# Row-block projection of the first K, the first Q in score banks, and P*V moved to the next score visit, in a fused attention and gated-MLP kernel

## The chip, the cores and the metric

One NeuronCore of one Trainium2 chip. The metric is the device time of one execution in microseconds (us), the median over runs. A profile covers one execution, and its span (first to last instruction) is about 1.8 us shorter than that run's device time.

Engines: PE is TensorE (matmuls), PEld its weight loads, ACT ScalarE, DVE VectorE, POOL GpSimd, SP the engine that issues most DMA. L449 in a line of the profile is line 449 of that kernel's source.

## The reference, cut to what matters

```python
def reference(A_x, A_wq, A_wk, A_wv, A_wo, A_beta, B_x, B_w_gate, B_w_up, B_w_down, gate_w):
    # x: 2048 x 512; 32 heads of 16; four segments of 512 tokens
    q, k, v = x @ wq, x @ wk, x @ wv
    for s in range(4):
        a_dot = softmax(qs @ ks.T * scale + mask) @ vs     # causal, inside a segment
        a_mem = phi(qs) @ M / (phi(qs) @ z + 1e-6)         # memory of earlier segments
        o = g * a_mem + (1 - g) * a_dot
        M, z = M + phi(ks).T @ vs, z + phi(ks).sum()
    a = concat(o) @ wo
    b = (gelu(x @ w_gate) * (x @ w_up)) @ w_down           # 512 -> 1792 -> 512
    gate = sigmoid((x * gate_w).sum(-1))
    return gate * a + (1 - gate) * b
```

## The kernel before

The program is recorded as tasks, and a list scheduler written in the kernel's own Python gives each engine its order when the program is built. It keeps a simulated clock per engine, fed with hand-written estimates and one bias per task name. On the chip there is only the finished order; semaphores enforce its dependencies. So an edit of an estimate or a bias can reorder the whole kernel.

PE does two kinds of work: plain matmuls on the whole array, and *tiled* ones, which split it into four row or column groups (32\*128, and 128\*17 or 128\*32, in the timelines). Scores (`qk`) and P*V (`pv`) are tiled, and so is the memory update (`mz`). A *visit* is a run of tiled matmuls between two plain ones; a *hole* is a stretch in which PE stands still.

```python
PATIENCE = 3.0                      # how long a P*V waits for a score visit to join
# ... loads of the head
for c0, c1 in ((0, 128), (128, 512)):
    for key, w, src in (("wk", wk, A_wk), ("wq", wq, A_wq)):
        wdma((key, c0 > 0), SP, w[:, :, c0:c1], r4(src)[:, :, c0:c1], ...)
wdma("wv", SP, wv[:], r4(A_wv), 524288)
wdma("gwb", SP, gwb[:], gate_w.partition_broadcast(P), 131072)
wdma("beta", SP, betab[:], A_beta.partition_broadcast(P), 65536)
wdma(("wg", 0), SP, wg[:, :, 0:half], ...)      # first half of the columns of w_gate
wdma(("wg", 1), SP, wg[:, :, half:DF], ...)     # second half
xdma(1)                             # x of segment 1, transposed by DMA, four pieces
for i in range(7):                  # matmuls on a constant, while x is on its way
    gw = Grp(banks)
    n = 512 if i < 6 else 384
    task(f"warm{i}", PE, [Instr(lambda e, gw=gw, n=n: e.matmul(
        gw.f32()[:, 0:n], ones[:, 0:128], ones[:, 0:n], start=True, stop=True),
        [], [gw.key], 0.107 * n / 128)], grp=gw, bias=5000.0 - i)
# ... memory(s): 64 small matmuls, the task mz{s}
m = task(f"mz{s}", PE, [Instr(... e.matmul(..., tile_position=(0, 32 * c))) 
                        for t in range(4) for kt in range(4) for c in range(4)], grp=gm)
m.tiled = "pv"
m.patience = PATIENCE
# ... attention(s): 32 small matmuls per P*V, two per tile t
p = task(f"pv{s}_{t}_{j}", PE, instrs, grp=gp, after=joint)
p.tiled = "pv"
p.patience = 0.0 if t == 3 else PATIENCE        # the last of a segment does not wait
# ... the program
xdma(2, after=pk0); wdma(("wu", 0), ...); wdma(("wu", 1), ...); wdma("wd", ...); wdma("wo", ...)
# ... the end
for t in S.schedule():
    for ins in t.alts[t.eng]:
        em.plan(t.eng, ins)
```

(Cuts are marked with "...".)

The softmax here doesn't subtract the row's maximum and nothing guards it: scores larger than these inputs give would overflow.

Of the kernel before, what the change touches and what calls it, by code (L numbers as in the profile page):

```python
# [32 lines left out]
PV_JOIN = 0.11  # L33
# [3 lines left out]
    "D0": -705, "D1": -805, "D2": -380, "D3": -442, "G0": -222, "G1": -900, "G2": -744, "G3": -86, "GdT0": 97,  # L37
    "GdT1": 844, "GdT2": -1, "GdT3": 895, "Gev0": 862, "Gev1": -349, "K0": 777, "K1": -529, "K2": 250,
    "K3": 307, "Q0": 715, "Q1": -519, "Q2": 584, "Q3": -641, "U0": -844, "U1": -888, "U2": -53, "U3": -206,
    "Um0": 900, "Um1": 148, "Um2": 49, "Um3": -86, "V0": 318, "V1": -357, "V3": 539, "Vev0": 540, "Vev1": 758,  # L40
    "Vev2": 262, "Vev3": -72, "Vlo0": -900, "Vlo1": 900, "Vlo2": -70, "Vlo3": 237, "consts": 21, "exp0": -666,
    "exp1": 177, "exp2": -517, "exp3": -395, "exsT0": 77, "exsT1": -899, "exsT2": -94, "exsT3": 695, "fin0": 37,
    "fin1": -471, "fin2": 741, "fin3": -517, "gbd": -146, "gelu0": -795, "gelu1": 416, "gelu2": 1, "gelu3": 126,
    "gexp": 402, "gexs0": -594, "gexs1": -701, "gexs3": 76, "gmat": -900, "gmul1": 900, "gmul2": -10,
    "gmul3": 319, "gsum0": -318, "gsum1": -86, "gsum2": -613, "gsum3": -900, "gts0": 73, "gts1": -850,
    "gts2": -487, "gts3": 848, "ident": 503, "kl0": -826, "kl1": -900, "kl2": -661, "kl3": 900, "kp0": 509,
    "kp1": 3, "kp2": -900, "kp3": -405, "masks": 769, "msk0": -290, "msk1": 789, "msk2": 116, "msk3": -63,
    "mz0": -162, "mz1": 638, "mz2": -319, "mzacc0": -423, "mzacc1": 170, "mzacc2": 439, "mzbd0": -25,
    "mzbd1": -178, "mzbd2": 70, "norm0": 704, "norm1": -880, "norm2": -46, "norm3": 166, "num2": -887,
    "num3": -200, "nump1": -900, "nump2": -220, "nump3": -164, "oTd1": 896, "oTd2": 268, "oTd3": 899,  # L50
    "omg": 528, "out0": 408, "out1": -644, "out10": 2, "out11": 869, "out12": 745, "out13": 461, "out14": -25,
    "out15": -280, "out2": 230, "out3": -27, "out4": 313, "out5": -134, "out6": 284, "out7": -18, "out8": 682,
    "out9": -139, "pkT0": 5, "pkT1": 569, "pkT2": 281, "pkc0": 489, "pkc1": -900, "pkc2": -14, "pke0": 310,
    "pke1": 399, "pke2": -73, "pqc1": 496, "pqc2": 14, "pqc3": -117, "pqe1": -17, "pqe2": 649, "pqe3": 63,
    "pv0": -95, "pv1": -551, "pv2": -900, "pv3": 30, "pvt0": -169, "pvt1": 86, "pvt2": -513, "pvt3": -26,
    "qk0": 417, "qk1": 185, "qk2": 503, "qk3": 669, "tload": 355, "vones": -877, "w": -765, "warm0": 21,
    "warm1": 747, "warm2": -324, "warm3": 371, "warm4": 223, "warm5": -120, "warm6": -334, "x0": -96,
    "x0ev0": 93, "x0ev1": 23, "x0t0": 596, "x0t1": 606, "x1": 367, "x2": -181, "x3": -900, "xt1": 533,
    "xt2": -189, "xt3": 11
# [42 lines left out]
class Task:  # L102


    def __init__(self, name, alts, grp=None, after=(), bias=0.0, nbytes=0):
        self.name = name
        self.alts = alts
        self.grp = grp
        self.after = tuple(after)
        self.bias = bias + BIAS.get(name[:re.search(r"[_.]|$", name).start()], 0.0)  # L110
        self.nbytes = nbytes
        self.tiled = None
        self.patience = 0.0
        self.ahead = False
        self.est = {e: sum(i.est for i in l) for e, l in alts.items()}
        rs, ws = set(), set()
        for l in alts.values():
            for i in l:
                rs.update(i.reads)
                ws.update(i.writes)  # L120
        self.reads, self.writes = rs, ws
        self.preds, self.succs = set(), set()
        self.prio = 0.0
        self.eng = None
        self.start = self.finish = None
        self.id = None


class Sched:
# [32 lines left out]
    def schedule(self):  # L162
# [34 lines left out]
        last_pe = None  # L197
        while len(order) < n:
# [34 lines left out]
            if e == PE:  # L233
                if t.tiled == "pv" and last_pe == "pv":
                    t.finish -= PV_JOIN
                last_pe = t.tiled
# [137 lines left out]
def _build(es, nc, A_x, A_wq, A_wk, A_wv, A_wo, A_beta, B_w_gate, B_w_up, B_w_down, gate_w, out):  # L374
# [108 lines left out]
    rank = [9000.0]  # L483
# [5 lines left out]
    def wdma(key, eng, dst, src, nbytes, nonc=False, after=()):  # L489
        rank[0] -= 20.0  # L490
        dma("w_" + str(key), eng, lambda: dst, lambda: src, [], [("w", key)], nbytes, bias=rank[0], nonc=nonc,
            after=after)

    def xdma(s, after=()):
        for kb in range(4):
            rank[0] -= 20.0
            dma(f"x{s}_{kb}", SP, lambda kb=kb: xT[s % NX][:, kb, :],
                lambda kb=kb: A_x[0, s * 512:(s + 1) * 512, kb * 128:(kb + 1) * 128],
                [], xk(s, kb), 262144, issue=1.25, transpose=True, bias=rank[0] if s < 2 else 0.0,
                after=after)  # L500
# [10 lines left out]
              [("c", "ident")], [("c", "ident")], 0.3)], bias=9990.0)  # L511
    task("tload", ACT, [Instr(lambda e: e.activation(stmp[:, 0:1], ones[:, 0:1], ACTF.Exp), writes=[("stmp",)],
                              est=1.5)], bias=8000.0)
    xin = hT[1][:, 0:4, :]
    for a in range(4):
        rank[0] -= 20.0
        dma(f"x0_{a}", (SP, ACT)[a % 2], lambda a=a: xin[:, a, :], lambda a=a: A_x[0, a * 128:(a + 1) * 128, :], [],
            [("hT", 1, a)], 131072, bias=rank[0], issue=0.45)
    for c0, c1 in ((0, 128), (128, 512)):
        for key, w, src in (("wk", wk, A_wk), ("wq", wq, A_wq)):  # L520
            wdma((key, c0 > 0), SP, w[:, :, c0:c1], r4(src)[:, :, c0:c1], 1024 * (c1 - c0) * (2 if c0 == 0 else 1))
    wdma("wv", SP, wv[:], r4(A_wv), 524288)
    wdma("gwb", SP, gwb[:], gate_w.partition_broadcast(P), 131072)
    wdma("beta", SP, betab[:], A_beta.partition_broadcast(P), 65536)
    wdma(("wg", 0), SP, wg[:, :, 0:half], wgr[:, :, 0:half], 917504)
    wdma(("wg", 1), SP, wg[:, :, half:DF], wgr[:, :, half:DF], 917504)
    xdma(1)
# [23 lines left out]
    for g in range(4):  # L551
# [6 lines left out]
                               writes=[("Vaug", i, kt) for kt in range(4)], est=2.3) for i in range(2)]  # L558
         + [Instr(lambda e, j=j: e.memset(Vlow[j][:], 0.0), writes=[("Vlow", j)], est=2.3) for j in range(2)],
# [47 lines left out]
    def proj_T(name, s, t, w, wkey, dst, wkeys, even=None):  # L607

        g = Grp(banks)
        xs = xT[s % NX]  # L610
        nu = 2 if even is not None else 1
        cols = [slice(512 // nu * u, 512 // nu * (u + 1)) for u in range(nu)]
        pieces(name, g, [mm(g, lambda c=c: g.f32()[:, c], w[:, kb, t * 128:(t + 1) * 128], xs[:, kb, c],
                            [*(xk(s, kb)[u:u + 1] if nu > 1 else xk(s, kb)), ("w", (wkey, t > 0))],
                            kb == 0, kb == 3, 512 // nu)
                         for u, c in enumerate(cols) for kb in range(4)], 2 * nu)
        if even is not None:
            task(name + "even", ACT, [Instr(lambda e: e.activation(even[0], g.f32()[:, :], ACTF.Copy,
                                                                   scale=maskc[0][:, 0:1]),
                                            [g.key, ("c", "mask", 0)], [even[1]], act_t(512, ap=True))], grp=g)  # L620
        copy_out(name + "ev", g, lambda: dst[:, t, :], lambda: g.f32()[:, :], [g.key], wkeys, 512)

    def phi_task(nm, s, phase, src, skey, dst, dkey, i):
# [13 lines left out]
                  dk + [("pex",)], dk, 0.95)])  # L637

    def klow_tasks(s, tiles):
# [3 lines left out]
        for j in range(2):  # L643
# [6 lines left out]
                            rd, wr, act_t(n, False, ap=True))],  # L650
                DVE: [Instr(lambda e, dst=dst, src=src, j=j: e.tensor_scalar(dst, src, maskc[j][:, 0:1], None, ALU.mult),
                            rd, wr, dve_t(n, 1, ap=True))]}))

    def prep(s):
# [21 lines left out]
        for tile in range(4):  # L676
            g = Grp(banks)
            pieces(f"V{s}_{tile}", g, [mm(g, lambda g=g: g.f32()[:, :], xT[x3][:, kb, tile * 128:(tile + 1) * 128],
                                          wv[:, kb, :], [*xk(s, kb), ("w", "wv")], kb == 0, kb == 3, 512)
# [4 lines left out]
        for j in range(2):  # L684
            dma(f"Vlo{s}_{j}", SP, lambda j=j: Vlow[j][j:P:2], lambda j=j: Vaug[sl][0:64, :, j],
                [("Vaug", sl, tile) for tile in range(4)], [("Vlow", j)], 139264)
# [8 lines left out]
        for a in range(4):  # L695
# [3 lines left out]
                            [("gprod", s)] + xkeys, [("glog", s, a), ("gjunk", s, a)], act_t(512, False) + 0.1)],  # L699
# [13 lines left out]
            exsT[sl][32 * g:32 * g + 32, c:16:4], exs[32 * c:32 * c + 32, s4]), [("exs", s), ek], [ek], 0.22)  # L713
# [81 lines left out]
    def attention(s):  # L795
        sl = s % 2
        for t in range(4):
            def fill(name, steps, dst, key, masks):

                instrs = []  # L800
                for (lhs, rhs, c0, ncol, rd) in steps:
                    for g in range(4):
# [3 lines left out]
                            (0.2 / len(steps) + ncol / 2370.0 + (0.01 if ncol < 128 else 0.0)) / 4))  # L806
# [27 lines left out]
            def lows(t=t):  # L834
# [8 lines left out]
                masks = [(PTl[:].rearrange("p g (b c) -> p (g b) c", c=64), [[0, 32], [2, 64]], 1, 2048)]  # L843
                fill("L", steps, PTl, ("PTl",), masks)

            def pv(j, where, joint):
                gp = Grp(banks)
                instrs = []
                for kb in range(4):
                    slot, c0 = where[kb]  # L850
                    for q in range(4):
# [4 lines left out]
                            [("PT", slot), ("Vaug", sl, kb)], [gp.key], 0.0342))  # L856
# [9 lines left out]
                p.patience = 0.0 if t == 3 else PATIENCE  # L866
# [3 lines left out]
            def norm():  # L870
# [11 lines left out]
                          [("recip", i2), ("GdT", sl)], [("sc1", i2)], 0.34),  # L882
# [3 lines left out]
                if s > 0:  # L886
                    ins.append(Instr(lambda e, t=t: e.tensor_tensor(oT[sl][:, t, :], oT[sl][:, t, :], ott[:],
                                                                    ALU.add), ok + dk, ok, 0.7))
# [240 lines left out]
```

## Time and profile before

| | before |
|---|---|
| device time, first 3 runs | 268.4, 269.25, 270.0 us |
| span of the profile | 267.5 us |
| plain 512-column matmuls, start to start | 0.216 us |
| first score visit starts | 16.84 us |
| last matmul ends | 264.87 us |

The waits of PE in the kernel before: who waited, for what, us in total, times, longest.

```profile
PE psW L449 <- issue: 3.8, 24, 0.2
...
PE psW L449 <- ACT qT L463: 0.4, 1, 0.4
PE psW L449 <- ACT hT L937: 0.4, 1, 0.4
...
PE psW L449 <- DMA wk<-in_A_wk_dram: 0.3, 1, 0.3
```

No wait of weight. The 24 of 0.2 us are gaps where a matmul was not recorded (2965 recorded, 3005 built).

The timeline of PE before, around two later points of interest: start, duration, line, operation, output and inputs, count, and in brackets the idle time ahead with its cause.

```profile
18.48 1.03 PE L449 MATMUL psW<-xT,wg 128*128 128x512 bf16 x4
19.43 0.40 PE L803 MATMUL psXALL<-qT,kpad 32*128 32x320 bf16 x8
19.99 2.11 PE L449 MATMUL psW<-xT,wg 128*128 128x512 bf16 x9 [0.16 <-issue]
...
27.23 0.40 PE L803 MATMUL psXALL<-qT,kpad 32*128 32x320 bf16 x8
27.56 0.71 PE L769 MATMUL psW<-vaug,phkt 128*32 128x34 bf16 x64
28.43 1.67 PE L449 MATMUL psW<-xT,wq 128*128 128x512 bf16 x7 [0.16 <-DVE phq L632]
...
33.06 0.40 PE L803 MATMUL psXALL<-qT,kpad 32*128 32x320 bf16 x8
33.39 0.61 PE L852 MATMUL psW<-pt,vaug 128*17 128x448 bf16 x16
...
34.83 1.24 PE L449 MATMUL psW<-xT,wg 128*128 128x512 bf16 x5 [0.16 <-issue]
```

Every visit closes within 0.2 us. The 64 memory matmuls (L769) come at 27.56, in another visit than the first P*V (L852 and L860) at 33.39.

### The profile page before, as it was taken

Reading aid. Unit: us, or ns where it says so; the run is one execution under the profiler, and the core shown is the slowest. Engines: PE = TensorE matmul, PEld = TensorE weight load, DVE = VectorE, ACT = ScalarE, POOL = GpSimd, SP = SyncE. Lnnn points to the kernel's source line nnn. Section 1 sums busy time; section 2 is a strip of 40 time slices with the busy share of each in tenths; the row PEclk is TensorE's granted clock in tenths of the full one; section 3 lists DMA queues with packets and bytes.
Section 4 is the critical chain, followed back from the end, with each engine's and each line's share of the span. In section 5 each row is a group of like instructions: output and inputs, shape, how many; then the busy total and the mean of one; then the engine's idle time right before and its main releaser. Section 6 shows DMA issues by size and latency. Waiting matters only on the chain.

```text
span 267.5 us, 7093 instructions
## 1 busy us (share of the span) xinstructions
PE 257.9 (96%) x2965; PEld 118.4 (44%) x3005; DVE 199.9 (75%) x385; ACT 212.1 (79%) x188; POOL 102.3 (38%) x232
## 2 busy tenths in 40 slices
PE   8999999999999999999999999999999999999996
PEld 5444444344443443434354444444344444444354
DVE  1769799898989898889756877987952688753451
ACT  4889988899998997998858998887767767777602
POOL 8364553873002433485201433486300252352300
PEclk9999999999999999999999999999999999999999
DMA  6998992000203443000021224010020025001002
GB/s 192 228 328 184 390 241 42 1 2 0 44 0 79 81 101 102 22 20 2 0 44 39 42 59 124 21 44 2 0 44 0 2 59 42 0 22 36 8 0 78
DMA packets 33775, 18.22 MB, mean 68 GB/s; under 512 B 21456, under 2 KB 33744, under 8 KB 33744
## 3 DMA queue, kind: packets, MB, share of 16 engines
q1 hardware_dynamic: 33456, 17.51, 27.0%
q8 instruction: 23, 0.38, 0.6%
q10 hardware_dynamic: 288, 0.26, 0.3%
q14 instruction: 8, 0.07, 0.1%
HBM read 9.84 MB, written 2.10 MB: 45 GB/s over the span
## 4 chain that ended last, share of the span: by engine, by line
PE 84%; ACT 5%; DVE 3%; issue 3%; DMA 2%; POOL 1%; SPq 0%; ACTq 0%; DVEq 0%
PE psW L449 68%; PE psXALL L803 8%; PE psW L852 5%; ACT pt L810 3%; DMA wk<-in_A_wk_dram 2%; PE psXALL L449 1%; PE psW L860 1%; POOL exsT L712 1%; DVE tb L867 0%; PE psW L769 0%; ACT L937 0%; ACT L926 0%; SPq L480 0%; DVE mzbd L784 0%; DVE phkt L692 0%
## 5 line engine op out<-in xcount | busy, mean ns | idle before, releaser
L810 ACT ACTIVATE pt<-psXALL 128x2048 bf16<-128x2048 f32 x64 | 120.1, 1876 | 26.0 <-PE psXALL L803 23.9
L814 POOL TENSOR_SCALAR_AFFINE_SELECT pt<-pt 128x256 bf16<-128x256 bf16 x128 | 59.2, 464 | 131.6 <-ACT pt L810 126.6
L449 PE MATMUL psW<-xT,wu 128*128 128x512 bf16 x216 | 51.9, 380 | 0.8 <-issue 0.6
L449 PE MATMUL psW<-xT,wg 128*128 128x512 bf16 x214 | 50.2, 380 | 1.7 <-issue 1.3
L449 PE MATMUL psW<-wd,hT 128*128 128x512 bf16 x203 | 50.3, 380 | 0.9 <-issue 0.8
L958 DVE TENSOR_TENSOR hT<-psW,hT 128x512 bf16<-128x512 f32 x56 | 37.5, 684 | 11.4 <-PE psW L449 10.9
L449 PEld LDWEIGHTS psW<-xT,wg 128*128 128x128 bf16 x224 | 20.4, 98 | 25.7 <-issue 2.5
L449 PEld LDWEIGHTS psW<-xT,wu 128*128 128x128 bf16 x224 | 20.4, 98 | 24.5 <-issue 2.3
L867 DVE STREAM_TRANSPOSE tb<-psW 128x512 f32<-128x512 f32 x32 | 21.3, 697 | 12.6 <-PE psW L860 12.2
L449 PEld LDWEIGHTS psW<-wd,hT 128*128 128x128 bf16 x210 | 18.8, 98 | 22.5 <-issue 2.5
L803 PE MATMUL psXALL<-qT,kpad 32*128 32x320 bf16 (+3 forms) x512 | 25.8, 273 | 0.3 <-ACT pt L810 0.3
L937 ACT ACTIVATE hT<-psW 128x512 bf16<-128x512 f32 x28 | 15.9, 601 | 7.0 <-PE psW L449 6.9
L814 POOL TENSOR_SCALAR_AFFINE_SELECT ptl<-ptl 128x2048 bf16<-128x2048 bf16 x8 | 16.9, 2117 | 9.4 <-ACT ptl L810 9.0
L803 PEld LDWEIGHTS psXALL<-qT,kpad 32*128 32x128 bf16 x512 | 7.7, 92 | 27.6 <-ACT pt L810 19.6
L852 PE MATMUL psW<-pt,vaug 128*17 128x192 bf16 (+3 forms) x512 | 18.7, 273 | 0.0
L810 ACT ACTIVATE ptl<-psXALL 128x2048 bf16<-128x2048 f32 x8 | 15.0, 1876 | 3.6 <-PE psXALL L803 3.6
L449 PE MATMUL psW<-xT,wk 128*128 128x512 bf16 (+1 forms) x64 | 16.1, 376 | 0.8 <-issue 0.5
L712 POOL COPY exsT<-exs 32x4 f32<-32x4 f32 x64 | 15.4, 241 | 3.7
L466 DVE CAST hT<-psW 128x512 bf16<-128x512 f32 x21 | 14.1, 683 | 2.8 <-PE psW L449 2.5
L449 PE MATMUL psW<-wo,oT 128*128 128x512 bf16 x55 | 15.2, 380 | 0.5 <-issue 0.3
L449 PE MATMUL psW<-xT,wq 128*128 128x512 bf16 x60 | 14.9, 380 | 0.7 <-ACT qT L463 0.4
L449 PE MATMUL psW<-wv,xT 128*128 128x512 bf16 x62 | 15.0, 380 | 0.3 <-issue 0.3
(98 smaller groups left out, 300.0 us busy)
## 6 DMA issues: line engine op xcount, KB each, us to landing
out_dram<-ost SPq DMA_DIRECT2D x15, 128.0 KB, 1.7
wg<-in_B_w_gate_dram SPq DMA_DIRECT2D x2, 896.0 KB, 6.1
wu<-in_B_w_up_dram SPq DMA_DIRECT2D x2, 896.0 KB, 5.9
wd<-in_B_w_down_dram SPq DMA_DIRECT2D x1, 1792.0 KB, 12.1
phkt<-in_A_x_dram SPq DMA_DIRECT2D x3, 512.0 KB, 4.1
vlow<-vaug SPq DMA_DIRECT2D x8, 136.0 KB, 2.9
wv<-in_A_wv_dram SPq DMA_DIRECT2D x1, 512.0 KB, 6.2
wo<-in_A_wo_dram SPq DMA_DIRECT2D x1, 512.0 KB, 9.7
```

The source lines that it names most:

```text
L449: return Instr(lambda e: e.matmul(view(), lhsT, rhs, start=first, stop=last), reads=reads, writes=[fkey if fkey is not None else g.key], e ...
L466: alts[DVE] = [Instr(lambda e: e.tensor_copy(dst(), src()), reads=reads, writes=writes, est=dve_t(n))]
L712: cross = task(f"exsT{s}", POOL, [Instr(lambda e, g=g, c=c: e.tensor_copy(exsT[sl][32 * g:32 * g + 32, c:16:4], exs[32 * c:32 * c + 32, s4 ...
L803: instrs.append(Instr(lambda e, g=g, lhs=lhs, rhs=rhs, c0=c0, ncol=ncol: e.matmul(X[g][:, c0:c0 + ncol], lhs(32 * g), rhs(32 * g), start=T ...
L810: prev_exp[0] = exp_task(s, f"exp{s}_{t}{name}", [Instr(lambda e: e.activation(dst[:], XALL[:, :].rearrange("p (g c) -> p g c", g=4), ACTF ...
L814: task(f"msk{s}_{t}{name}", POOL, [Instr(lambda e, view=view, pat=pat, base=base: e.affine_select(out=view, in_=view, compare_op=ALU.is_ge ...
L852: instrs.append(Instr(lambda e, t=t, q=q, kb=kb, slot=slot, c0=c0: e.matmul(gp.f32()[32 * q:32 * q + 17, 128 * kb + 64:512], Vaug[sl][:, k ...
L860: instrs.append(Instr(lambda e, t=t, q=q, kb=kb, c0=c0: e.matmul(gp.f32()[32 * q:32 * q + 17, 128 * kb:128 * kb + 64], Vlow[j][:, kb, 4 * ...
L867: task(f"pvt{s}_{t}_{j}", DVE, [Instr(lambda e: e.transpose(Tb[:, j, :], gp.f32()[:, :]), [gp.key], [("Tb", j)], dve_t(512))], grp=gp)
L937: lambda e, g=g, ft=ft, s=s: e.activation(hT[s % 2][:, ft, :], g.f32()[:, :], ACTF.Gelu_apprx_tanh),
L958: task(f"Um{s}_{ft}", DVE, [Instr(lambda e, g=g, ft=ft: e.tensor_tensor(hT[sl][:, ft, :], g.f32()[:, :], hT[sl][:, ft, :], ALU.mult), [g.k ...
```

## The change

It loads wk as four blocks of 128 rows over two queues, and projects the first K block by block over all four column tiles. The first Q goes to the four score banks, which are idle then. The last P*V of a segment waits for the next score visit instead of making its own. The mask on `ptl` is split in four, estimates are set to measured times, the scheduler charges 0.097 us for each change of tiling mode (joining a P*V to a score visit saves 0.098 us by the trace before: 0.642 + 1.751 - 2.082 - 0.213), and biases can be given per task, all of them new. So the whole order is new. The core of the diff (the long tables of biases and the estimates are cut):

```diff
-PV_JOIN = 0.11
+SWITCH = 0.097
@@
-                if t.tiled == "pv" and last_pe == "pv":
-                    t.finish -= PV_JOIN
-                last_pe = t.tiled
+                if t.tiled != mode:
+                    t.finish += SWITCH
+                mode = last_pe = t.tiled
@@
-    for c0, c1 in ((0, 128), (128, 512)):
-        for key, w, src in (("wk", wk, A_wk), ("wq", wq, A_wq)):
-            wdma((key, c0 > 0), SP, w[:, :, c0:c1], ...)
-    wdma("wv", SP, wv[:], r4(A_wv), 524288)
+    for kb in range(4):
+        wdma(("wk", kb), (SP, ACT)[kb % 2], wk[:, kb, :], A_wk[128 * kb:128 * kb + 128, :], 131072)
+    for key, w, src in (("wq", wq, A_wq), ("wv", wv, A_wv)):
+        for i in range(2):
+            wdma((key, i), SP, w[:, 2 * i:2 * i + 2, :], r4(src)[:, 2 * i:2 * i + 2, :], 262144)
+    xdma(1)
+    wdma("beta", SP, betab[:], A_beta.partition_broadcast(P), 65536)
     wdma("gwb", SP, gwb[:], gate_w.partition_broadcast(P), 131072)
-    wdma("beta", SP, betab[:], A_beta.partition_broadcast(P), 65536)
     wdma(("wg", 0), SP, wg[:, :, 0:half], wgr[:, :, 0:half], 917504)
     wdma(("wg", 1), SP, wg[:, :, half:DF], wgr[:, :, half:DF], 917504)
-    xdma(1)
@@ proj_T
+        head = s == 0
+        x = head and wkey == "wq"
+        view = (lambda: X[t]) if x else (lambda: g.f32()[:, :])
+        nu = 2 if head and wkey == "wk" else 1
@@
-                p.patience = 0.0 if t == 3 else PATIENCE
+                p.patience = (PATIENCE, 30.0 if s < NSEG - 1 else 0.0)[t == 3]
```

In the built order of PE, tiled visits went from 76 to 73.

## The prediction

> **What bounds the kernel now.** TensorE: the page gives PE 257.9 of 267.5 us (96%), ACT 212.1, DVE 199.9, POOL 102.3. Busy is not peak, so I measured start-to-start distances in the trace: between ordinary (untiled) 512-column matmuls it is 0.216 us from 7.2 us to the end. The waits of PE sum to 6 us, of which 3.8 us are 24 "issue" waits that match unrecorded matmuls (2965 recorded, 3005 built). Nothing holds PE up by over 0.5 us after 7.2 us. Beside plain work there are:
> 1. Head (timeline, 0 to 10 us): warm-up and 16 transposes to 5.45 us; eight 256-column K matmuls, most 0.213 us apart, twice their later pace, until about 6.4 us; a wait for the rest of wk, issued 2.2, landed 7.2 us. K ends at about 9.83.
> 2. Tiled visits. A lone score visit costs 0.642 us from the ordinary matmul before to the one after; score plus both P*V 2.082; both P*V alone 1.751. Joining saves 0.642 + 1.751 - 2.082 - 0.213 = 0.098 us: one change of tiling mode.[...]
> 3. Tail: last matmul ends at 264.87; eviction and output take 2.6 us more.

> **What the change does.** The built order has the same matmul work (12 512-column K matmuls become 24 of 256). Lone P*V visits go from four to one, tiled visits from 76 to 73: -0.3 us. In the head, wk comes as four row blocks with 1 KB rows on two queues; block kb of all column tiles can run once it landed. x landed at 3.4 to 4.2 us and the DMA then moves some 350 GB/s with 1 KB rows, so (estimate) wk lands at 4.6 to 5.8 us instead of 7.2. K starts at 5.45, at half pace to about 6.4, and ends at about 9.4 instead of 9.83: -0.4 us.[...] Q in score banks frees work banks for V, but PE did not wait for them before; it only guards against evictions, dense on ACT from 7 to 16 us. V needs K's banks evicted by about 9.5 to 10.3 us; some 0.2 us of stall may come back there. Split masks, new estimates and biases move work on ACT, DVE, POOL, which wait for PE anyway: worth nothing unless PE is made to wait.

> **On the critical path:** both savings; the chain of waits is 84% PE. Sum -0.7 us, less perhaps 0.1 to 0.3 of new short waits from a wholly reshuffled order.

> **Predicted** 268.6 us, range 267.0 to 270.0. Chances: faster by over 2% 0.03, within 2% 0.93, slower 0.04.

> **What would show each step.** Right: wk landed before 6 us, no DMA wait of PE at 7; last K matmul about 9.4; first score visit within 0.3 us of 16.8; three fewer lone P*V visits, joined ones still 2.08 us; ordinary matmuls still 0.216 us apart; last matmul some 0.7 us earlier, tail 2.6 us. Wrong: PE waits for wv or wq near 9.5, for evictions near 10, or for a gelu or exp in mid kernel.

> **What would make it wrong.** Stalls of PE in the gelu stretches or at full work banks, which the order cannot show (slower);[...] wv late behind the new DMA order. Over 2% faster would need 5.4 us of PE work or waits to vanish, and no such waits are there.

-0.3 us for the joined P*V and -0.4 us for the head make the -0.7 us, and -0.6 to -0.4 us with the new waits. That the half pace would stay until about 6.4 us was the estimate from the kernel before, where the first K matmuls were 0.213 us apart until 6.46 us. The 350 GB/s is read there too: 338 and 358 GB/s in the two stretches from 7 to 9 us, when 1 KB rows of wv moved, mixed with shorter ones.

## More of the kernel before

Lines of the profile's page for the kernel before: span and instructions; busy us with share of the span and count; two rows in 40 slices (busy tenths of PE, and the granted PE clock in tenths); the PE instruction queue (packets, MB, share of the DMA engines' time); and the chain of waits by engine.

```profile
span 267.5 us, 7093 instructions
PE 257.9 (96%) x2965; PEld 118.4 (44%) x3005; DVE 199.9 (75%) x385; ACT 212.1 (79%) x188; POOL 102.3 (38%) x232
...
PE   8999999999999999999999999999999999999996
...
PEclk9999999999999999999999999999999999999999
...
q8 instruction: 23, 0.38, 0.6%
...
PE 84%; ACT 5%; DVE 3%; issue 3%; DMA 2%; POOL 1%; SPq 0%; ACTq 0%; DVEq 0%
```

PE is busy throughout and owns the chain. Note q8: 23 packets in the whole run.

## The result, and the profile after

Before 268.4, 269.25, 270.0, 268.46 us (median 268.86); changed 277.36, 279.09, 277.55, 278.67 us (median 278.11). The ratio is 1.034, 95% interval 1.029 to 1.039: slower by 3.4%. Ratios here are the mean time of one kernel's runs over that of the other's of the same rounds, so not quite the ratio of the medians quoted.

The four changed executions are not alike. Their granted PE clock, averaged over the run, was 0.994, 0.988, 0.987 and 0.981. In the profiled one, the fastest, the clock record shows one stretch at half clock, of 3.41 us (39.20 to 42.61 us), which lowers the mean by 0.006. So the other three had two or three such stretches (an estimate), and the profile shows somewhat less than the typical loss: 8.1 us of span, against 9.25 us between the medians.

The same lines of the page for the changed kernel:

```profile
span 275.6 us, 7171 instructions
PE 264.4 (96%) x3017; PEld 119.9 (44%) x3017; DVE 197.4 (72%) x387; ACT 212.3 (77%) x186; POOL 107.8 (39%) x256
...
PE   7997959999999999999999999999999999999996
...
PEclk9999989999999999999999999999999999999999
...
q8 instruction: 23, 0.38, 0.6%
...
PE 72%; POOL 6%; ACT 5%; issue 5%; SPq 4%; DMA 4%; DVE 4%; ACTq 0%; POOLq 0%; DVEq 0%
```

PE is still "96% busy", so that figure hides the loss. The rows in slices show it: a 7 in the fourth slice and a 5 in the sixth (34 to 41 us), where the clock dips too.

The largest waits of PE in the changed kernel:

```profile
PE psXALL L861 <- issue: 3.5, 2, 3.1
PE psW L501 <- DMA wg<-in_B_w_gate_dram: 1.8, 1, 1.8
PE psW L501 <- DMA wk<-in_A_wk_dram: 0.9, 2, 0.7
...
PE psW L501 <- DVE hT L1017: 0.7, 2, 0.5
```

The longest wait is put down to "issue": PE waited for nothing that the profile shows. The timeline of PE at both places:

```profile
19.99 0.40 PE L861 MATMUL psXALL<-qT,kpad 32*128 32x320 bf16 x8
22.24 1.04 PE L501 MATMUL psW<-xT,wg 128*128 128x512 bf16 x4 [1.85 <-DMA wg<-in_B_w_gate_dram]
...
32.30 0.40 PE L861 MATMUL psXALL<-qT,kpad 32*128 32x448 bf16 x8
32.63 0.72 PE L827 MATMUL psW<-vaug,phkt 128*32 128x34 bf16 x64
33.23 0.62 PE L911 MATMUL psW<-pt,vaug 128*17 128x448 bf16 x16
33.66 0.30 PE L919 MATMUL psW<-ptl,vlow 128*17 128x64 bf16 x16
33.77 0.62 PE L911 MATMUL psW<-pt,vaug 128*17 128x448 bf16 x16
...
34.98 0.39 PE L861 MATMUL psXALL<-qT,kpad 32*128 32x320 bf16 x5
38.48 0.26 PE L861 MATMUL psXALL<-qT,kpad 32*128 32x192 bf16 x3 [3.11 <-issue]
38.67 4.45 PE L501 MATMUL psW<-xT,wg 128*128 128x512 bf16 x12
```

Read the last three lines closely. A score visit is eight matmuls, and the built order has no wait after the first of them. PE did five, stood still for over 3 us, and did the other three. And the 12 plain matmuls after it took 4.45 us, not 2.8.

The stretches after and before that place: busy us of PE, PEld, DVE, ACT and POOL with counts; then the granted PE clock, the DMA share (the packets' times summed, over 16 engines' time; it can pass 1) and GB/s. First the changed kernel:

```profile
34.90:38.90 4.00, 0.89 (x10) 0.32 (x10) 1.32 (x2) 0.92 (x2) 3.26 (x14) 1.00 1.63 324
38.90:42.90 4.00, 4.00 (x12) 1.40 (x10) 2.58 (x6) 2.02 (x2) 1.60 (x7) 0.57 0.96 110
```

Then the kernel before:

```profile
34.40:38.40 4.00, 3.84 (x51) 1.67 (x40) 3.87 (x9) 3.48 (x4) 1.87 (x6) 1.00 1.29 272
38.40:42.40 4.00, 3.84 (x32) 1.54 (x32) 3.87 (x7) 3.54 (x5) 1.66 (x4) 1.00 1.06 103
```

After the hole the granted clock was 0.57 for 4 us (before: 1.00). One matmul then took 0.34 and seven took 0.427 us start to start instead of 0.216.

**Where 8.1 us of span went**, from start-to-start distances in the two traces. Each is the excess over the usual distance:

| | us |
|---|---|
| wait for w_gate at 20 us | 1.90 |
| hole at 35 us | 3.27 |
| half pace after the hole | 1.60 |
| second hole, 171 us (0.57 + 0.16), less two of 0.16 in the kernel before | 0.41 |
| waits for evictions and masks in mid kernel, 2.4 against about 1.5 | 0.9 |
| head: first score visit 17.40 with two more plain matmuls ahead of it (0.43), against 16.84 | 0.13 |
| three joined P*V | -0.3 |
| sum | 7.9 |

That leaves 0.2 us unassigned.

```
page 1 (asked for at about instruction 466)        before     changed
PE issues instruction 466                          27.96 us   32.73 us
packet 1 starts to move                            31.86      36.07
  ... instructions issued by then                  540        705
packet 1 has moved                                 32.79      37.00
PE reaches instruction 705                         35.5       35.13, stops
PE goes on                                         -          38.48
```

(The counts before are low by up to 40, as it lacks that many records.) The packet waited 3.9 us in the kernel before too, while the transfers of w_up, w_down and wo ran at 389 GB/s (28 to 33 us; that it waits behind them is tested below). Elsewhere packets start within about 3 us of that point, before or after, as the point is itself an estimate; 14 of the other 22 in the changed kernel come 0.2 to 1 us after it. But in the kernel before PE took 7.5 us over the 240 instructions it still held. In the changed kernel most of them belong to one visit of 272 instructions (score, memory and both P*V), and the 240 were gone in 2.4 us. The second hole, at 171 us, comes 3,072 instructions after the first: 12 pages exactly.

The first hole lies at a count and not at a piece of work. In every run below that has one, PE stops between its recorded instructions 701 and 705: among score matmuls in tests 2, 3 and 5, between two plain ones in test 4, and inside a P*V in test 7.

So PE stopped about 240 instructions after the estimated asking point (466 to 705), for 3.3 us. How many pages PE can hold ahead is not shown.

This is still a reading of traces. The experiments test it.

### The profile page after: what moved, and what is told of

The parts are those of the page before. It is cut to its first block, busy times and chain, and to the rows that moved or that the text cites. A ratio compares the mean times of both kernels' runs of the same rounds, so it can differ in the third digit from the quotient of the medians.

```text
span 275.6 us, 7171 instructions
## 1 busy us (share of the span) xinstructions
PE 264.4 (96%) x3017; PEld 119.9 (44%) x3017; DVE 197.4 (72%) x387; ACT 212.3 (77%) x186; POOL 107.8 (39%) x256
## 4 chain that ended last, share of the span: by engine, by line
PE 72%; POOL 6%; ACT 5%; issue 5%; SPq 4%; DMA 4%; DVE 4%; ACTq 0%; POOLq 0%; DVEq 0%
PE psW L501 57%; PE psXALL L861 7%; PE psW L911 5%; DMA wg<-in_B_w_gate_dram 4%; POOL exsT L770 4%; ACT pt L868 3%; SPq L528 2%; SPq L532 2%; PE psXALL L501 1%; POOL ptl L872 1%; PE psW L919 1%; POOL pt L872 1%; DVE hT L1017 1%; DVE kpad L730 1%; PE psW L827 1%
## 5 line engine op out<-in xcount | busy, mean ns | idle before, releaser
L872 POOL TENSOR_SCALAR_AFFINE_SELECT pt<-pt 128x256 bf16<-128x256 bf16 x128 | 57.0, 447 | 127.1 <-ACT pt L868 122.3
L501 PE MATMUL psW<-xT,wg 128*128 128x512 bf16 x224 | 53.8, 389 | 1.8 <-DMA wg<-in_B_w_gate_dram 1.8
L501 PE MATMUL psW<-xT,wu 128*128 128x512 bf16 x224 | 53.9, 380 | 0.3 <-DVE hT L1017 0.3
L501 PE MATMUL psW<-wd,hT 128*128 128x512 bf16 x210 | 51.5, 380 | 0.0
L1017 DVE TENSOR_TENSOR hT<-psW,hT 128x512 bf16<-128x512 f32 x56 | 36.9, 685 | 4.8 <-PE psW L501 4.2
L872 POOL TENSOR_SCALAR_AFFINE_SELECT ptl<-ptl 128x512 bf16<-128x512 bf16 x32 | 22.7, 711 | 11.5 <-ACT ptl L868 9.6
L518 DVE CAST hT<-psW 128x512 bf16<-128x512 f32 x20 | 13.5, 682 | 6.8 <-PE psW L501 6.5
L770 POOL COPY exsT<-exs 32x4 f32<-32x4 f32 x64 | 16.7, 261 | 3.7
L501 PE MATMUL psW<-wo,oT 128*128 128x512 bf16 x60 | 15.8, 380 | 0.0
L1069 DVE TENSOR_SCALAR ost<-psW,omgt 128x512 bf16<-128x512 f32 x8 | 6.0, 746 | 11.7 <-PE psW L501 11.6
```

The costliest lines, as they stand in the source:

```text
L501: return Instr(lambda e: e.matmul(view(), lhsT, rhs, start=first, stop=last), reads=reads, writes=[fkey if fkey is not None else g.key], e ...
L518: alts[DVE] = [Instr(lambda e: e.tensor_copy(dst(), src()), reads=reads, writes=writes, est=dve_t(n))]
L770: cross = task(f"exsT{s}", POOL, [Instr(lambda e, g=g, c=c: e.tensor_copy(exsT[sl][32 * g:32 * g + 32, c:16:4], exs[32 * c:32 * c + 32, s4 ...
L872: task(f"msk{s}_{t}{name}", POOL, [Instr(lambda e, view=view, pat=pat, base=base: e.affine_select(out=view, in_=view, compare_op=ALU.is_ge ...
L1017: task(f"Um{s}_{ft}", DVE, [Instr(lambda e, g=g, ft=ft: e.tensor_tensor(hT[sl][:, ft, :], g.f32()[:, :], hT[sl][:, ft, :], ALU.mult), [g.k ...
L1069: DVE: [Instr(lambda e, view=view, gt=gt, tile=tile: e.tensor_scalar(ostage[tile % N_OST][:], view(), omgt[:, gt:gt + 1], None, ALU.mult), rd,
```

## Experiments

Theory: the hole is a late page of PE instructions, made by a burst of instructions against a fetch stuck behind weight transfers. The wait at 20 us is (b) and (c). The half pace follows from PE standing still. Rivals: a hidden wait for data or buffers; the new head; the new order as such; or weight transfers alone.

Most edits change the finished order alone, through this helper at the end of the build, so that no scheduler reshuffles anything:

```python
order = S.schedule()
def move(names, ahead_of):        # these tasks to just ahead of another, nothing else
    got = [t for t in order if t.name in names]
    rest = [t for t in order if t.name not in names]
    at = next(i for i, t in enumerate(rest) if t.name == ahead_of)
    order[:] = rest[:at] + got + rest[at:]
```

All twelve kernels gave right results. The kernel before ran in every set (medians 269.08, 269.27, 269.40 and 269.31 us); the changed kernel ran in the first test alone, so "against 278.11" compares across sets.

Half pace also differs between executions of one kernel. In tests 1, 5, 6, 9 and 10 some ran at a granted clock of 0.993 or 0.994 and the others at 0.999 to 1.00; on average the first took 1.3 to 2.6 us longer. So a median of four to six runs can move by that much with no change of cause, and the waits read in the traces are firmer than the totals.

### 1. Forty-eight tiny matmuls in the warm-up

```diff
 for i in range(7):
+    if i in (2, 3, 4):            # 16 tiny ones in place of one of 512 columns
+        body = [Instr(lambda e, gw=gw: e.matmul(gw.f32()[0:16, 0:32], ones[:, 0:16], ones[:, 0:32], ...),
+                      [], [gw.key], 0.107 * n / 128 / 16) for _ in range(16)]
```

> The changed kernel with three of its seven warm-up matmuls replaced by 48 tiny ones; nothing else moves. That puts about 90 more TensorE instructions before the first real work, so every 256-instruction page of the TensorE stream begins about 90 instructions of work earlier. Theory (instruction fetch): the 3.3 us hole at 35 us comes where a page of TensorE instructions had not arrived; with the pad the second page is asked for about 5 us earlier in the work, so the hole shrinks under 0.6 us and the half-pace stretch after it (1.7 us) goes: 273.2 us, range 272 to 275, against 278.1 for the changed kernel. Rival (a data or buffer wait, or the new order itself): no data, order or wait of other engines has changed, so the hole stays over 2.5 us and the time stays 277.5 to 279.

Measured: 271.6 us (270.7 to 273.9), ratio 1.011 (1.006 to 1.016). The timeline of PE there:

```profile
31.36 0.71 PE L833 MATMUL psW<-vaug,phkt 128*32 128x34 bf16 x64
...
33.41 0.38 PE L501 MATMUL psW<-xT,wg 128*128 128x512 bf16 x1 [0.16 <-issue]
33.72 0.40 PE L867 MATMUL psXALL<-qT,kpad 32*128 32x320 bf16 x8
34.05 2.76 PE L501 MATMUL psW<-xT,wg 128*128 128x512 bf16 x12
```

The same visit, burst and transfers, and no hole: all eight score matmuls in one go, then 12 plain ones in 2.76 us instead of 4.45. The page was now asked for at 28.4 and had moved by 30.2 us. The order of the real work was the same, and only the place of the page borders in it had changed (and the head, whose first score visit came 0.35 us earlier), so a hidden data wait is out. The time was 0.4 us better than the low end expected; the wait for w_gate was also shorter, 0.98 us. A wait of 0.85 us for an eviction at 44.4 us (DVE hT) was new.

### 2. w_down and wo transferred later

```diff
+    move(['w_wd', 'w_wo'], 'msk0_1B1')     # after x of segment 2, on the DMA queue alone
```

> The changed kernel with the DMA of wd and wo issued after those of x for segment 2, with the same order on all compute engines. Theory (instruction fetch queued behind the weight transfers): the page that started 3.3 us after it was asked for now starts within 1 us of it; the hole at 35 us shrinks from 3.3 us to under 1 us, the half-pace stretch goes, 273.2 us, range 272 to 275. Rival (the burst of joined P*V and memory matmuls outruns the fetch whatever the DMA does): hole over 2 us, time over 276.

Measured: 274.85 us (274.6 to 275.1), ratio 1.021 (1.020 to 1.023).

```profile
36.53 0.78 PE L861 MATMUL psXALL<-qT,kpad 32*128 32x320 bf16 x8
37.24 2.76 PE L501 MATMUL psW<-xT,wg 128*128 128x512 bf16 x12
```

The hole shrank to 0.29 us and its half pace went, with the burst in place. The packet moved 0.4 us after it was due, not 3.3. So the burst alone does not make the hole; the rival is out. The total was at the upper end of the range, for a reason I had not foreseen: in this profile the wait for w_gate at 20 us (1.93 us) was followed by half pace, from 22.93 to 26.35 us in the clock record. All four executions had a clock of 0.993 or 0.994.

### 3. The second half of w_gate first

```diff
+    move(["w_('wg', 1)"], "w_('wg', 0)")
```

> The changed kernel with the second half of w_gate transferred ahead of the first, since the new order uses columns of the second half first. Theory: the wait of 1.9 us for w_gate at 20 us goes, as the half that is used first then lands near 19.5 us; the hole at 35 us stays: 276.2 us, range 275.3 to 277. Rival (whatever PE gains there is lost at the next limit, such as the hole, which is set by when the weight transfers end): 277.5 to 278.5.

Measured: 275.3 us (274.6 to 277.5), ratio 1.022 (1.019 to 1.024). The largest waits of PE (two, of 3.6 us and the rest):

```profile
PE psXALL L861 <- issue: 4.2, 2, 3.6
```

No wait for w_gate is left. The hole at 35 us was there, 3.72 us, with 12 matmuls slowed after it. (This profile is of the slowest of five executions, 277.47 us at a clock of 0.987; the other four had 0.994.) So the wait was the order of the halves, and the hole did not take the gain back. The gain of 2.8 us, across sets, is more than the wait of 1.9 us; fewer half-pace stretches may be the rest, which is not shown.

### 4. The joined visit put into the kernel before

```diff
+    move(['mz0', 'mzacc0', 'xt1'], 'qk0_1B0')     # in the kernel before; nothing else of the change
```

> The kernel before, with the 64 memory matmuls of segment 0 moved one score visit later, so that they, the score and both P*V stand in one visit (272 instructions without a pause), as in the changed kernel. Nothing else of the change is in it. Theory (burst of instructions against a fetch delayed by weight transfers): a hole of 2 to 4.5 us appears in PE after that visit, near 35 us, with a half-pace stretch of up to 1.8 us: 273.5 us, range 271.5 to 275.5, against 268.9. Rival (holes come from the head, the mask splits or the new biases): no hole, 268.5 to 269.5.

Measured: 270.64 us (270.3 to 270.8), ratio 1.006 (1.004 to 1.007). The size was missed, the kind was not:

```profile
32.31 0.70 PE L769 MATMUL psW<-vaug,phkt 128*32 128x34 bf16 x64
...
34.72 0.59 PE L449 MATMUL psW<-xT,wg 128*128 128x512 bf16 x2 [0.16 <-issue]
36.48 0.82 PE L449 MATMUL psW<-xT,wg 128*128 128x512 bf16 x3 [1.17 <-issue]
```

A hole of 1.33 us, where the kernel before had none, again put down to "issue", now between two plain matmuls. It was smaller because the packet waited 1.6 us, not 3.3: it was due at 32.45, nearer to the end of the weight transfers. No half pace followed. A second new hole, of 0.6 us at 102 us, ended 1.40 us after a later packet had moved. The time lies below the expected range and above the rival's.

### 5. beta and gwb ahead of x

```diff
+    move(['w_beta', 'w_gwb'], 'x1_0')
```

> The changed kernel with the DMA of beta and gwb issued ahead of the four transposed loads of x for segment 1 (about where the kernel before has them), nothing else moved. Theory: in the changed kernel the DMA queue runs empty from 12 to 15 us because gwb, and w_gate behind it, come after the four slow transposes; with gwb early, both halves of w_gate land as in the kernel before (about 17 and 19.3 us, not 19.5 and 22.2), the 1.9 us wait at 20 us goes, the hole at 35 us (3.3 to 3.7 us) and the half pace after it stay: 275.8 us, range 274.5 to 277. Rival (gwb is slow wherever it stands[...], and w_gate lands late all the same): wait over 1.2 us, 277.5 to 279.

Measured: 274.01 us (272.9 to 274.75), ratio 1.017 (1.014 to 1.020), 0.5 us below the range. Two of the waits of PE:

```profile
PE psXALL L861 <- issue: 3.0, 1, 3.0
...
PE psW L501 <- DMA wg<-in_B_w_gate_dram: 0.2, 1, 0.2
```

gwb landed at 10.9 instead of 17.2 us, the two halves of w_gate at 16.8 and 19.7 instead of 19.5 and 22.2, and the wait at 20 us fell to 0.24 us. So undoing either this or the order of the halves is enough to remove the wait. The hole (3.14 us) stayed.

### 6. The memory matmuls taken out of the joined visit

```diff
+    move(['mz0', 'mzacc0', 'xt1'], 'qk0_1A1')     # in the changed kernel
```

> The changed kernel with the 64 memory matmuls of segment 0 moved out of the joined visit to one and a half visits later, beside another score. Theory (burst against fetch): the page boundary is met about 2.4 us later, while the fetch is asked for about 0.5 us later, so the hole shrinks from 3.3 us to 0.5 to 1.8 us, and the half-pace stretch shrinks or goes: 275.0 us, range 273.5 to 276.8. Rival (the hole belongs to the weight transfers alone and ends when they end): hole over 2.5 us, 277 to 279.

Measured: 273.7 us (272.45 to 275.2), ratio 1.017 (1.013 to 1.021). The largest wait of PE after the gaps of unrecorded matmuls:

```profile
PE psW L501 <- DMA wg<-in_B_w_gate_dram: 1.9, 1, 1.9
```

The hole at 35 us was gone altogether, where 0.5 to 1.8 us was expected: PE came to instruction 705 at about 39.6 us, 4.5 us later and not 2.4, and the page had moved by 37.5. The wait for w_gate (1.92 us) was again followed by a half-pace stretch. With tests 2 and 4: it takes both, burst and busy DMA.

In all runs with a hole at this place, PE went on 1.4 to 1.6 us after the packet had moved (so too at the later, smaller holes, near 102 us in test 4 and near 170 us elsewhere: 1.40 to 1.56 us):

```
                     packet 1 has moved    PE goes on    difference
changed kernel       37.00                 38.48         1.48
late weights         35.63                 37.05         1.42
wg half first        35.85                 37.28         1.43
joined, before       35.02                 36.48         1.46
gwb first            34.41                 35.88         1.47
pad and wg half      30.71                 32.30         1.59
```

### 7 and 8. Both repairs, and a control

The changed kernel with edits 1 and 3, and the kernel before with edit 1.

> The changed kernel with both repairs, the 48 tiny warm-up matmuls and the second half of w_gate first. Theory: neither the wait at 20 us nor the hole at 35 us is left; what remains against the kernel before are PE waits for evictions in mid kernel, some 2 us: 270.4 us, range 269.4 to 271.4. Rival (a further cause not seen yet): over 272.

> Control: the kernel before with the same 48 tiny warm-up matmuls. Theory: it has no hole of over 0.4 us to lose, so the pad is worth nothing by itself: 268.7 us, range 268.0 to 269.6. Rival (the pad speeds any kernel[...]): under 267.

Measured: both repairs 270.6 us (270.2 to 271.1), ratio 1.005 (1.004 to 1.007). The control 268.64 us (268.5 to 268.8), ratio 0.998 (0.996 to 0.999). So the two named causes hold some 7.5 of the 9 us (across sets), the half pace that followed them included. A small hole of 0.6 us was left at 31.7 us, where a page border now fell into the P*V. The control shows that the pad does not speed up a kernel that has no such hole. Its 0.2% is at the edge of what these rounds resolve. It lost its two hiccups of 0.16 us, but its first score visit also came 0.43 us earlier, and which of these counts is open.

### 9, 10 and 11. More of it

Test 9 has the changed kernel with 96 tiny matmuls (six of the seven warm-ups) and edit 5; test 10 has edit 6 as well; test 11 is the kernel before with 96.

> The changed kernel with six of its seven warm-up matmuls replaced by 96 tiny ones (about 180 more TensorE instructions ahead of the first real work) and beta and gwb transferred ahead of x for segment 1. Theory: no wait for w_gate at 20 us over 0.3 us, no hole near 35 us at all, no half pace after the head; what is left over the kernel before are evictions in mid kernel, about 2.2 us in both, against 0.3 us saved by joined P*V: 268.4 us, range 267.6 to 269.4. Rival (the changed order costs 1 us or more by itself): over 269.8.

> The same, with the memory matmuls of segment 0 moved out of the joined visit as well. Theory: with the page there in time the joined burst costs nothing any more, so taking it apart only adds mode changes (0.1 us): 268.5 us, range 267.7 to 269.5, no faster than the run without it. Rival (the burst itself costs time): faster than that run by 0.5 us or more.

> The kernel before with the 96 tiny warm-up matmuls. Theory: like the control with 48, it loses its two fetch hiccups of 0.16 us and little else: 268.6 us, range 268.0 to 269.3. Rival[...]: K in the head at half pace beyond 7 us, over 269.5.

Measured: 271.53 us (270.4 to 273.5), 270.73 us (269.9 to 272.95) and 269.1 us (268.5 to 269.4); ratios 1.008, 1.006 and 0.998 (0.997 to 1.000). No hole near 35 us in any of the three. But tests 9 and 10 missed their ranges; in the profiles the loss is at the head. The waits and the timeline of PE in test 9:

```profile
PE psW L501 <- DMA wk<-in_A_wk_dram: 2.2, 1, 2.2
...
7.38 4.88 PE L501 MATMUL psW<-xT,wk 128*128 128x256 bf16 x28 [2.18 <-DMA wk<-in_A_wk_dram]
```

wk landed at 7.3 to 8.1 us, and then K ran at half pace until 10.9 us. (This profile is of one of two executions in six with a clock of 0.993 or 0.994, at 273.4 and 273.5 us; the other four, at 1.00, took 270.4 to 271.75 us. In the profile of test 10 wk landed at 6.8 to 7.7 us and no half pace followed.) PE's first page moved at 5.0 us in this run, amid wk (10.2 us in test 1), and from then on each load landed late on the slowest of the 16 parts in which it reports ("rings" in the expectation of test 12): wk block 0 was done on the first at 4.6 and on the last at 7.25 us. From first to last took 2.1 to 2.7 us for the blocks of wk in tests 9 and 10, and 0.6 to 1.95 us in the changed kernel and tests 1, 5 and 12. That the page delayed it is a guess and not shown. In the kernel before (test 11) the first page moved at 7.95 us and wk was not late. Tests 9 and 10 differ by 0.8 us, inside their spread, so they don't settle whether the burst costs something by itself.

### 12. Forty-eight, gwb first, unjoined

> The changed kernel with 48 tiny warm-up matmuls (not 96), beta and gwb ahead of x for segment 1, and the memory matmuls of segment 0 out of the joined visit. The run with 96 fetched its first page at 5.0 us, amid the transfer of wk, and all of wk, wq and wv landed about 2 us late on their slowest ring; with 48 that fetch falls near 10 us, after wk. Theory: wk lands by 7.2 us, first score visit by 17.2 us, no wait over 0.3 us for w_gate, no hole near 35 us; what is left are the evictions in mid kernel of the new order, 2.2 us: 268.8 us, range 268.0 to 269.8. Rival (the new order costs over 1 us by itself, whatever its holes): over 270.

Measured: 270.22 us (269.7 to 270.7), ratio 1.003 (1.001 to 1.005). It lies 0.4 us above its range, and 0.2 us beyond the mark of the rival (over 270), so the rival was nearer: with all its named losses repaired, the new order still costs about 0.9 us. No wait for w_gate, no hole. In the profile wk landed at 7.2 us as expected, and the first score visit came at 17.83, not 17.2. Repaired, the changed order is 0.3% slower than the kernel before, not faster. This one profile, counted as in the table, gives 0.56 us for the head (17.83, less 0.43 for the two more plain matmuls, against 16.84), 1.2 us for waits in mid kernel (2.7 against about 1.5) and -0.3 us for joined P*V. That makes 1.5 us, where its span is 1.4 us longer.

The only versions below the kernel before in these rounds are the kernel before with the pad, tests 8 and 11, by 0.2% each.

## Why the prediction was wrong, point by point

- **What bounds the kernel: right.** PE. Plain matmuls stayed 0.216 us apart outside the half-pace stretches, and each loss above is PE standing or running slowly.
- **Joined P*V, -0.3 us: right in kind.** Four lone visits became one, and with all records there a joined visit takes 1.855 us. The "2.08" that I expected held an unrecorded matmul. The lone visit held one too, so the 0.10 us per join comes out the same.
- **Head, -0.4 us: did not come.** I took 350 GB/s and had wk landed by 5.8 us; the trace gives 218 to 330 GB/s in the stretches from 4 to 7 us, and its blocks landed at 5.4, 5.6, 6.8 and 6.95 us. The last K matmul started at 9.86 (before: 9.62). Nearly the same head gave 9.04 in test 5, so the gain may show in one execution and not in another.
- **The step that failed** reads "less perhaps 0.1 to 0.3 of new short waits from a wholly reshuffled order". That term measured about +8 us, by three things: 1.9 us for w_gate, 3.3 us for a page of instructions, 1.6 us of half pace, besides the smaller ones in the table. The half pace is in part chance: an execution can have more of it or less (granted clock 0.981 to 0.994 in the four of the changed kernel). I had compared the order of the DMA issues and looked for wv, and did not look up *which half* of w_gate the first gate matmul needs, though the built order names the semaphore. The instruction page I did not think of: no line of the profile before shows it as a wait, as the kernel before happened to have 7.5 us of work in hand.
- "Nothing holds PE up by over 0.5 us" was true of the kernel before and said nothing about its margins. The fetch was 3.9 us late there as well.
- **Worth nothing unless PE is made to wait** (masks, estimates, biases): the condition was met (2.4 us of such waits in mid kernel against about 1.5). Their separate shares were not tested.
- The prediction had half pace in the head alone, as the kernel before shows it there (256-column K matmuls 0.213 us apart until 6.46 us, then 0.11). In the changed kernel's head they were 0.108 us apart from the first, at 5.57 us; half pace came in mid kernel instead, after PE had stood still for 3.1 us: 512-column matmuls 0.427 us apart, with the granted clock at half from 39.20 to 42.61 us. What sets it is not shown.

What stays open: why gwb took 3.8 us to move (12.99 to 16.84 us) in the changed kernel and 1.0 us in the kernel before; why half pace follows a wait of 1.9 us in one execution and not in another (1.93 and 1.92 us in tests 2 and 6 were followed by it, 1.90 us in the changed kernel was not); and whether the repaired order's 0.9 us can be won back.

## What to carry to other kernels

A trace shows who waited, not how much slack there was: before joining small matmuls into one visit, count the instructions in the burst, find where the pages of PE's instructions fall (256 in each here, by the 256.2 a packet above), and see what DMA is in flight when the next is due. A gap in PE with the cause "issue", in the middle of a group that has no wait, with an instruction packet ending 1.4 to 1.6 us before PE goes on, was a late page here; shifting the borders by some tiny matmuls, or moving a bulk load, tests it without touching anything else. When a scheduler reorders a kernel, check for each first use of a load which part it needs, and whether that part is the one that lands first.
